# ScalarE fills a block's third PSUM bank before it copies the chain bank, two slopes move behind later additions, and one nested sum of w_in moves to the front

## The chip, the cores and the metric

The kernel runs on one core of a Trainium2 chip. A core has a matrix engine (TensorE, "PE" in the profile, with its weight loads shown apart as "PEld"), a vector engine (VectorE, "DVE"), a scalar engine (ScalarE, "ACT"), GpSimd ("POOL") and a queue engine (SyncE, "SP"). Each works through its own list of instructions in order; they wait for one another through semaphores. The metric is the time of one execution on the device in microseconds (us). Lower is better.

## The reference, cut to what matters

An attention whose mask comes from hash buckets makes `x`. A two-layer network with a leaky slope per hidden feature follows; that second part is what the change touches.

```python
# attn_out: softmax of q k^T / 8 where the 6-bit hash buckets of q and k agree, times v
x = attn_out.transpose(0, 2, 1, 3).reshape(3072, 512)
h = x @ w_in                                         # 512 -> 2048
g = np.maximum(h, 0.0) + alpha * np.minimum(h, 0.0)
return (g @ w_out).astype(np.float32)                # 2048 -> 512
```

`alpha` lies between 0 and 0.3, so `g` is the larger of `h` and `alpha * h`. In the kernel that is one VectorE instruction, called a slope below.

## The kernel before, in words

**Two parts.** The attention runs first, up to about 317 us into the profile. Then the two matrix products of the network run for four batches `b = 0..3` of 768 tokens. A hand-written loop over `blocks` (line 1598) takes, for each batch, eight blocks of kind "1" (the hidden layer, two feature tiles of 128 per block) and seven of kind "2" (the output layer). `do(...)` keeps instructions in the order in which the Python calls them, so the calls in this loop are the queues of the engines.

**Seven products in place of eight.** Each matrix product is cut 2 x 2 and computed with seven products of sums (a Strassen-like scheme). The class `Product` (line 906) holds one block. Its tiles are named by block and bank: `f_3a`, `f_3c` in the profile are PSUM banks "a" and "c" of hidden block 3, `f_3u` the SBUF copies of its chain, `z_7a` a bank of the output layer. Bank "a" is a chain: products are added on top of one another, and between two of them ScalarE copies the bank out (`keep`).

**Batches 1 to 3 nest the scheme.** There, three of the seven products of the hidden layer are computed for four blocks at once and once more by seven products. The class `Inner` (line 1105) does the first two (tiles `na` to `nf`, results `n`), the class `Third` (line 1172) the third (tiles `n_2a`, `n_2b`, `n_2c`; results straight into `g`). `unit(b, u, before)` (line 1248) runs both `Inner` products for blocks `4u..4u+3`. What is left of each block are four products, in the class `Rest` (line 1015). Its banks do not start at zero: ScalarE writes a first value into them, called a seed here.

**The steps of a `Rest` block**, each one call of `step`:

- step 1: ScalarE seeds bank "a" (one block ahead).
- step 6: PE adds a product to bank "a" (four matmuls, 384 wide); ScalarE copies it to tile `u1`.
- step 5: ScalarE seeds bank "c". PE does nothing.
- step 3: PE adds a product to bank "c", which needs the seed; VectorE adds "c" to `u1` in place (line 992) and takes the slope of the sum in place into `g` (line 996, reading `u1`), then one difference of `g` (line 977).
- step 7: PE adds to bank "a" (after the `u1` copy has been read out), ScalarE copies to `u2`, VectorE adds and takes a slope.
- step 4: PE adds the last product to "a"; ScalarE copies to `h`; VectorE takes the slope and one difference.

There is one buffer for bank "c" (its own PSUM pool) and one buffer for tile `u1`. So block n may seed "c" when VectorE's line 992 has read the "c" of block n-1, and may copy `u1` when VectorE's line 996 of block n-1 has read the old `u1`. At a block's change the loop calls

```python
                now = after
                now.step(6)
                third(b1, n1, "6")
                now.step(5)
                before.step(4)
```

which gives ScalarE the order: copy `u1`, copies of `Third`, seed "c", copy `h`. PE's order is step 6, `Third`, step 4 of the block before, then step 3.

**`Third`** is spread over the blocks by the table `THIRD` (line 1237). For blocks 4 to 7 its last step, 4, falls at the change to block 5; its VectorE work is one addition and `slopes(1)`, two slopes on `g` (line 1203).

**Sums of w_in.** The nested products need sums of quarters of `w_in` (`sum_inner`, line 1086: four additions, each followed by a store to DRAM on POOL's queue) and differences of quarters of `x` (`sum_inner_x`, line 1094: three). The sums of `w_in` are computed in batch 1 alone; later batches load them. In `unit` for `u = 0` VectorE's order is: three differences of `x`, then four sums of `w_in` (tiles `wp`), of which the second `Inner`'s step 5 (`nf<-xn,wp`) needs the first.

Of the kernel before, what the change touches and what calls it, by code (L numbers as in the profile page):

```python
# [407 lines left out]
def fast_path(  # L408
# [674 lines left out]
                do(nc.sync.dma_start(n_w[b, u, 2, 3 + m], w_n_s[u, 2, :, m]))  # L1083
            n_w[b, u, 2, 3 + m] = n_w[b, u, 2, 3 + m].rearrange("p (t f) -> p t f", t=2)

    def sum_inner(b, u, o):

        if b != 1:
            return
        for m, x, op, y in ((3, 21, ALU.add, 2), (4, 3, ALU.subtract, 0), (5, 0, ALU.subtract, 21), (6, 1, ALU.subtract, 4)):  # L1090
            do(DVE.tensor_tensor(n_w[b, u, o, m], n_w[b, u, o, x], n_w[b, u, o, y], op=op))
            nc.gpsimd.dma_start(w_n_s[u, o, :, m - 3].rearrange("p (t f) -> p t f", t=2), n_w[b, u, o, m])

    def sum_inner_x(b, o):

        x = x_m[b, (0, 3, 1)[o]]
        home = late[0] if o else mid
        t = home.tile([P, 4, HC], F32, name=f"xn{b}_{o}", tag=("x", "gs5", "m5")[o], bufs=1)
        left, right = (x[:, :, c * HC : (c + 1) * HC] for c in range(2))
        do(DVE.tensor_tensor(t[:, :2], right, x[:, 0].rearrange("p (c w) -> p c w", c=2), op=ALU.subtract))  # L1100
        do(DVE.tensor_tensor(t[:, 2], right[:, 1], t[:, 0], op=ALU.subtract))
        do(DVE.tensor_tensor(t[:, 3], left[:, 1], t[:, 2], op=ALU.subtract))
        n_x[b, o] = {0: left[:, 0], 1: left[:, 1], 2: right[:, 1], 3: t[:, 0], 4: t[:, 2], 5: t[:, 1], 6: t[:, 3]}
# [68 lines left out]
    class Third(Inner):  # L1172
# [30 lines left out]
                do(DVE.scalar_tensor_tensor(h, h, slope(i, False), h, op0=ALU.mult, op1=ALU.max))  # L1203

        def step(self, n):
            if n == 1:
                self.ps["a"] = two_banks(self.name + "a")[:, 0]
                self.ps["b"] = psum_bc[0].tile([P, 512], F32, name=self.name + "b", tag="b")
                self.times("a", 0, 0, True)
                do(ACT.copy(self.ps["b"][:, :CW], self.ps["a"][:, :CW]))  # L1210
            elif n == 2:
                self.times("b", 1, 1, False)
                self.add(0, 0, self.bank("b"))
            elif n == 6:
                self.times("a", 4, 4, False)
                self.keep("a", "u1")
                self.add(0, 1, self.sb["u1"])
            elif n == 5:
                self.ps["c"] = psum_bc[0].tile([P, 512], F32, name=self.name + "c", tag="b")
                self.times("c", 3, 3, True)  # L1220
                self.keep("c", "p5")
                self.add(1, 1, self.sb["p5"])
            elif n == 7:
                self.times("a", 5, 5, False)
                self.keep("a", "u2")
                self.add(1, 1, self.sb["u2"], self.to(1, 1))
            elif n == 3:
                self.times("c", 6, 2, False)
                self.add(0, 1, self.bank("c"), self.to(0, 1))
                self.slopes(0)  # L1230
            elif n == 4:
                self.times("a", 2, 6, False)
                self.add(1, 0, self.bank("a"))
                self.slopes(1)

    thirds = {}
    THIRD = (
# [4 lines left out]
    def third(b, i, place):  # L1242

        n = THIRD[i // 4].get((i % 4, place))
        if n:
            thirds[b, i // 4].step(n)

    def unit(b, u, before):

        def bank(name, tag=None):  # L1250
            name = f"n{name}{b}_{u}"
            return psum_bc[0].tile([P, 512], F32, name=name, tag=tag) if tag else two_banks(name)[:, 0]

        one = Inner(b, u, 0, bank("a"), bank("b", "b"), bank("c"))
        one.step(1)
        one.step(5)
        before.step(4)
        one.step(2)
        if not u:
            sum_inner_x(b, 1)  # L1260
        one.step(6)
        if not u:
            sum_inner(b, 0, 1)
            sum_x(b, 3, DVE)
        two = Inner(b, u, 1, bank("d"), bank("e", "b"), bank("f", "c"))
        two.step(1)
        one.step(3)
        two.step(5)
        one.step(7)
        if u:  # L1270
            sum_inner(b, 1, 2)
            sum_w2(b, 0, 3, 4)
        two.step(2)
        two.step(6)
        three = thirds[b, u] = Third(b, u)
        if u:
            three.step(1)
        one.step(4)
        two.step(3)
        if u:  # L1280
            three.step(2)
        now = ff1(b, 4 * u)
        now.step(1)
        two.step(7)
        now.step(6)
        now.step(5)
        two.step(4)
        three.step(6 if u else 1)
        if u:
            sum_w2(b, 0, 6, 5)  # L1290
        turn_out()
        if not u:
            sum_inner_x(b, 2)
            sum_inner(b, 0, 2)
        return now
# [302 lines left out]
    for j, (b, what, n) in enumerate(blocks):  # L1598
        n2 = n + 1 if what == "2" else 0 if n == NI - 1 else 7
        if n2 == 0:  # L1600
            sides_g(b, 0)
            if b == 0:
                sum_w2(b, 0, 3, 4)
        if not j:
            now.step(6)
        elif not (b and what == "1"):
            now.step(2)
        if j == 0:
            now.step(3)
            now.step(7)  # L1610
            now.step(2)
        if what == "2" and n == 6 and b + 1 < B:
            sum_inner(b + 1, 0, 0)
        now.step(22)
        if (b, what, n) == (1, "2", 1):
            largest()
        if what == "2" and b + 1 < B and 2 <= n < 6:
            if n == 3:
                sum_inner_x(b + 1, 0)
            else:  # L1620
                sum_x(b + 1, {2: 0, 4: 1, 5: 2}[n], DVE)
        if b and what == "1" and n == 1:
            load_inner(b, 1)
        if b and what == "1" and n == 2:
            load_third(b, 1)
        if b and what == "1" and n in (2, 3):
            sum_inner(b, 1, n - 2)
        if 0 < n2 < 7:
            sides_g(b, n2)
            sum_w2(b, n2, 3, 4)  # L1630
        if n2 < 7:
            sum_g2(b, n2, 3, 4)
        if j:
            if not (b and what == "1"):
                now.step(5)
                now.step(6)
            now.step(3)
            if b and what == "1":
                third(b, n, "3")
            if n2 or b == 0:  # L1640
                sum_w2(b, n2, 6)
            if b and what == "1" and (n + 1) % 4:
                after = ff1(b, n + 1)
                after.step(1)
            now.step(7)
            if b and what == "1":
                third(b, n, "7")
            if n2 or b == 0:
                sum_w2(b, n2, 5)
            sum_g2(b, n2, 5)  # L1650
        if (b, what, n) == (1, "2", 3):
            verdict()
        if what == "2" and n < 2:
            sum_g(1 + n)

        for n_out in [(), (0,), (1,), (2, 3), (4,), (5, 6), (7,)][j] if j < 7 else ():
            sum_out(n_out)
        for n_out in [(1,), (2, 3), (4,), (5, 6), (7,)][j] if j < 5 else ():
            load_out(n_out)
        if what == "1":  # L1660
            load_w(b * NI + n + 3)

            if b and n in (2, 5):
                load_w2(b, n // 4)
            if not b and n >= NI - 2:
                load_w2(b, n - NI + 2)
        else:
            load_w2(b, n + 2)
            if b + 1 < B:
                if n == 5:  # L1670
                    load_inner(b + 1, 0)
                    load_third(b + 1, 0)
                if n == 0:
                    load_x(b + 1)
        if j + 1 == len(blocks):
            turn_last(0)
        elif what == "1" or n < 6:
            turn_out()
        before = now
        if j + 1 < len(blocks):  # L1680
            b1, what1, n1 = blocks[j + 1]
            if b1 and what1 == "1" and n1 % 4 == 0:
                now = unit(b1, n1 // 4, before)
            elif b1 and what1 == "1":
                now = after
                now.step(6)
                third(b1, n1, "6")
                now.step(5)
                before.step(4)
                third(b1, n1, "4")  # L1690
            else:
                now = ff1(b1, n1) if what1 == "1" else ff2(b1, n1)
                now.step(1)
                before.step(4)
        else:
            before.step(4)
        if n2 < 7:
            sum_g2(b, n2, 6)
# [29 lines left out]
```

## Time and profile before

| what | value |
|---|---|
| median of 3 runs | 862.58 us (862.37 to 862.63) |
| the profiled execution | 862.93 us |
| its span in the trace | 861.1 us |
| granted PE clock | 0.998 of full speed |
| PE busy from 475 to 520 us (blocks 3 to 7 of batch 1) | 43.74 of 45.00 us |
| PE busy from 610 to 655 us (the same of batch 2) | 44.75 of 45.00 us |
| PE busy from 745 to 790 us (the same of batch 3) | 44.75 of 45.00 us |
| DVE busy in the same three stretches | 40.54, 37.91, 37.94 us |
| ACT busy in the same three stretches | 19.60, 20.51, 19.85 us |

The span runs from the first recorded instruction to the last; the execution takes 1.8 us more than it. The page gives no chain of waits for this kernel, so the argument has to come from the waits, the timeline and the starts of matmuls. Busy times of PE are modelled from starts and shapes; starts are recorded.

### The profile page before, as it was taken

What the parts mean: (1) busy time and instruction counts of PE and PEld (TensorE: products, weight loads), DVE (VectorE), ACT (ScalarE), POOL (GpSimd) and SP (SyncE); (2) the same over time, 40 slices, a digit from 0 to 9 for tenths busy, and PEclk for the clock granted to TensorE, in tenths of its full rate; (3) what the DMA queues carried; (4) which work ended last, traced back from release to release, by engine and by line L of the source; (5) the groups of instructions that cost most, each with busy time, mean ns of one, the idle gap of its engine ahead of it and who ended that gap; (6) DMA issues with size and microseconds to landing.
All of it is one profiled execution on the core that took longest, in us unless ns stands there. A gap on an engine that the chain in (4) does not pass through costs nothing.

```text
span 861.1 us, 15383 instructions
## 1 busy us (share of the span) xinstructions
PE 848.1 (98%) x5674; PEld 598.6 (70%) x5674; DVE 770.9 (90%) x1251; ACT 407.7 (47%) x754; POOL 154.5 (18%) x321
## 2 busy tenths in 40 slices
PE   8999999999999999999999999999999999999996
PEld 4444444444444445569997769999777999687996
DVE  6999999999999987899997989997879998879986
ACT  7777888877778833331124442114442114352111
POOL 1322433324334310210016200002100000300001
PEclk9999999999999999999999999999999999999999
DMA  8965779879597437774444744335833335830252
GB/s 197 180 149 132 187 177 251 170 197 256 131 241 194 154 117 258 250 260 176 148 151 122 271 135 136 110 118 177 290 125 113 144 117 171 264 115 20 99 166 60
DMA packets 181765, 144.85 MB, mean 168 GB/s; under 512 B 121536, under 2 KB 161648, under 8 KB 178096
## 3 DMA queue, kind: packets, MB, share of 16 engines
q1 hardware_dynamic: 166496, 113.15, 46.3%
q0 software_dynamic: 12176, 29.29, 11.2%
q10 hardware_dynamic: 3008, 1.33, 0.6%
q8 instruction: 47, 0.77, 0.4%
q14 instruction: 38, 0.31, 0.1%
HBM read 111.16 MB, written 31.46 MB: 166 GB/s over the span
## 4 chain that ended last, share of the span: by engine, by line


## 5 line engine op out<-in xcount | busy, mean ns | idle before, releaser
L790 ACT ACTIVATE pt<-sc 128x768 f32<-128x768 f32 x192 | 153.9, 813 | 3.2 <-PE sc L787 3.0
L787 PE MATMUL sc<-qT,kT 64*128 64x384 f32 x768 | 155.0, 482 | 0.0
L820 PE MATMUL av<-pt,vn 128*32 128x385 f32 (+1 forms) x1536 | 127.0, 485 | 0.0
L820 PEld LDWEIGHTS av<-pt,vn 128*32 128x32 f32 x1536 | 50.3, 109 | 73.8 <-issue 68.8
L787 PEld LDWEIGHTS sc<-qT,kT 64*128 64x128 f32 x768 | 68.2, 187 | 37.8 <-issue 37.6
L1407 POOL DMA_DIRECT2D out_dram<-o x52 | 28.3, 552 | 339.7 <-DVE o L1400 338.2
L787 PE MATMUL sc<-qb,kb 64*128 64x384 bf16 x384 | 63.0, 324 | 0.7 <-DVE alpha L563 0.4
L977 DVE TENSOR_TENSOR g<-g,g 128x768 f32<-128x768 f32 (+1 forms) x80 | 62.7, 792 | 0.7
L1353 DVE TENSOR_TENSOR gs<-g,gs 128x768 f32<-128x768 f32 x56 | 53.2, 951 | 1.0
L1353 DVE TENSOR_TENSOR gs<-g 128x768 f32<-128x768 f32 x56 | 53.2, 950 | 0.0
L1345 DVE TENSOR_TENSOR ws<-wl 128x512 f32<-128x512 f32 x56 | 38.3, 684 | 6.7 <-DMA wl<-w_out_s 6.7
L787 PEld LDWEIGHTS <-kb 64*128 64x128 bf16 x384 | 19.4, 94 | 34.9 <-issue 11.9
L607 ACT ACTIVATE wr<-raw 128x512 int32<-128x512 uint32 x32 | 22.1, 690 | 30.6 <-DVE wso L651 15.3
L748 POOL DMA_DIRECT2D qb<-hr x60 | 30.0, 507 | 25.9 <-ACT hr L743 25.9
L798 DVE TENSOR_TENSOR accp<-pt,pt 128x1536 f32<-128x1536 f32 x16 | 28.1, 1756 | 7.2 <-ACT pt L790 7.2
L996 DVE SCALAR_TENSOR_TENSOR g<-h,alpha 128x384 f32<-128x384 f32 x39 | 23.9, 613 | 6.4 <-ACT h L989 6.4
L803 DVE TENSOR_TENSOR accd<-accd,pt 128x1536 f32<-128x1536 f32 x16 | 28.1, 1759 | 1.7
L809 DVE TENSOR_TENSOR accd<-accd,accp 128x1536 f32<-128x1536 f32 x16 | 28.1, 1758 | 0.6
L806 DVE TENSOR_TENSOR accp<-accp,pt 128x1536 f32<-128x1536 f32 x16 | 28.0, 1753 | 0.0
L802 DVE TENSOR_TENSOR accd<-pt,pt 128x1536 f32<-128x1536 f32 x16 | 28.0, 1751 | 0.0
L1557 ACT ACTIVATE qT<-qT 128x768 f32<-128x768 f32 x15 | 12.7, 844 | 25.3 <-DMA kb<-hr 20.8
L1365 DVE TENSOR_TENSOR m<-m,m 128x768 f32<-128x768 f32 x24 | 22.7, 945 | 0.3
(494 smaller groups left out, 1903.9 us busy)
## 6 DMA issues: line engine op xcount, KB each, us to landing
wi<-w_in_s SPq DMA_DIRECT2D x32, 512.0 KB
wl<-w_out_s SPq DMA_DIRECT2D x16, 1024.0 KB
wl<-w_out_r SPq DMA_DIRECT2D x12, 1024.0 KB
raw<-in_moe_w_in_dram POOLq DMA_DIRECT2D x15, 512.0 KB, 5.1
raw<-in_moe_w_out_dram POOLq DMA_DIRECT2D x14, 512.0 KB, 4.8
w_in_s<-wsi SPq DMA_DIRECT2D x16, 448.0 KB
qn<-in_q_dram SPq DMA_DIRECT2D x64, 96.0 KB
vn<-in_v_dram SPq DMA_DIRECT2D x16, 384.0 KB
```

The source lines that it names most:

```text
L748: queue.dma_start(bits[name, pi][D * s : D * s + 2 * NB, half * CW : (half + 1) * CW], raw[c : c + 2 * NB],)
L787: do(PE.matmul(sc[:, s, :CW], what["k", pi][r, ks], what["q", pi][r, qs], start=first, stop=not first,))
L790: do(ACT.activation(pts[kc][:, g, :, :CW], sc[:, :, :CW], AF.Exp, scale=SCALE / DOWN))
L798: do(DVE.tensor_tensor(accp[pi], p(0), p(1), op=ALU.add))
L802: do(DVE.tensor_tensor(accd[pi], p(3), p(4), op=ALU.add))
L803: do(DVE.tensor_tensor(accd[pi], accd[pi], p(5), op=ALU.add))
L809: do(DVE.tensor_tensor(accd[pi], accd[pi], accp[pi], op=ALU.add))
L820: do(PE.matmul(av[pi][D * s + t : D * s + t + 32, g, :w], nat["v", pi][:, s, kc * D + t : kc * D + t + 32], pts[kc][:, g, s, :w], start=(k ...
L977: do(DVE.tensor_tensor(new_g(b, to)[:, at], g_m[b, x][:, at], g_m[b, y][:, at], op=ALU.subtract))
L1345: do(DVE.tensor_tensor(t, w2[b, n, x], w2[b, n, y], op=op))
L1353: do(DVE.tensor_tensor(t, g2[b, n, x], g2[b, n, y], op=ALU.subtract))
L1407: pinned(b + 1 < B and queue is nc.sync, queue.dma_start(out_v[b, ch * CH + c].rearrange("(w r) d -> r w d", r=32)[:, :, cols], src[32 * a ...
```

## The change

The function `sum_inner` takes a choice of sums, and `sum_inner_x` takes something to do after its first difference. In `unit` for `u = 0` the order on VectorE becomes: first difference of `x`, first sum of `w_in` (and its store on POOL's queue), the other two differences, the other three sums.

In `Third.step(4)` the two slopes are called for blocks 0 to 3 alone. For blocks 4 to 7 the loop calls them after step 7 of block 5, that is behind block 5's two additions (line 992), their slopes and one difference.

Steps 5 and 6 are exchanged at the change of every block but the first of four, and in `unit` for the first: ScalarE seeds "c" and then copies `u1`. PE's order stays.

```diff
-    def sum_inner(b, u, o):
+    def sum_inner(b, u, o, *ms):
...
         for m, x, op, y in ((3, 21, ALU.add, 2), (4, 3, ALU.subtract, 0), (5, 0, ALU.subtract, 21), (6, 1, ALU.subtract, 4)):
+            if ms and m not in ms:
+                continue
             do(DVE.tensor_tensor(n_w[b, u, o, m], n_w[b, u, o, x], n_w[b, u, o, y], op=op))
...
-    def sum_inner_x(b, o):
+    def sum_inner_x(b, o, between=lambda: None):
...
         do(DVE.tensor_tensor(t[:, :2], right, x[:, 0].rearrange("p (c w) -> p c w", c=2), op=ALU.subtract))
+        between()
         do(DVE.tensor_tensor(t[:, 2], right[:, 1], t[:, 0], op=ALU.subtract))
...
             elif n == 4:
                 self.times("a", 2, 6, False)
                 self.add(1, 0, self.bank("a"))
-                self.slopes(1)
+                if not u:
+                    self.slopes(1)
...
         if not u:
-            sum_inner_x(b, 1)
+            sum_inner_x(b, 1, lambda: sum_inner(b, 0, 1, 3))
         one.step(6)
         if not u:
-            sum_inner(b, 0, 1)
+            sum_inner(b, 0, 1, 4, 5, 6)
...
         two.step(7)
+        now.step(5)
         now.step(6)
-        now.step(5)
         two.step(4)
...
                 third(b, n, "7")
+                if n == 5:
+                    thirds[b, 1].slopes(1)
...
                 now = after
+                now.step(5)
                 now.step(6)
                 third(b1, n1, "6")
-                now.step(5)
                 before.step(4)
```

More of the change, by code (lines that the diff above doesn't have):

```diff
@@ L1205, in step @@
         def step(self, n):
+            b, u, o = self.key
             if n == 1:
```

## The prediction

> **What bounds the kernel now.** I read the page's busy times first, then PE's waits, then the timeline around each wait. The page:
>
> ```profile
> PE 848.1 (98%) x5674; PEld 598.6 (70%) x5674; DVE 770.9 (90%) x1251; ACT 407.7 (47%) x754; POOL 154.5 (18%) x321
> ```
>
> PE is busy nearly throughout, so what can be won without removing a product is only where PE stands still. PE's waits from 420 us on, in full:
>
> ```profile
> PE f_3c L928 <- ACT f_3c L1020: 1.0, 1, 1.0
> PE f_6c L928 <- ACT f_6c L1020: 0.8, 3, 0.3
> PE z_7a L928 <- DMA wl<-w_out_s: 0.4, 1, 0.4
> PE nf L1122 <- DVE wp L1091: 0.4, 1, 0.4
> PE z_4c L928 <- DVE m L1374: 0.2, 1, 0.2
> ```
>
> Columns: total, times, longest. Three of the five are what the change is about: seed "c" of block 3 (in batch 1 only), seed "c" of block 6 (once in each of batches 1 to 3), and the sum `wp` (batch 1). The times are too small, since PE's busy ends are modelled past the next start. The starts in the timeline give the loss. Block 3 of batch 1:
>
> ```profile
> 479.02 1.55 DVE L1091 TENSOR_TENSOR wn<-wn 128x256 f32<-128x256 f32 x4
> 480.23 1.45 PE L928 MATMUL f_2a<-x,wi 128*128 128x384 f32 x4
> 480.49 0.55 DVE L992 TENSOR_TENSOR f_2u<-f_2u,f_2c 128x384 f32<-128x384 f32 x1
> 481.07 0.62 DVE L996 SCALAR_TENSOR_TENSOR g<-f_2u,alpha 128x384 f32<-128x384 f32 x1
> 481.77 0.48 ACT L935 COPY f_3u<-f_3a 128x384 f32<-128x384 f32 x1 [2.10 <-PE f_2a L928]
> 482.15 0.49 ACT L1020 COPY f_3c<-n 128x384 f32<-128x384 f32 x1
> 482.69 1.56 PE L928 MATMUL f_3c<-x,wi 128*128 128x384 f32 x4 [1.01 <-ACT f_3c L1020]
> ```
>
> and block 6 of batch 1:
>
> ```profile
> 509.07 1.15 DVE L1203 SCALAR_TENSOR_TENSOR g<-g,alpha 128x384 f32<-128x384 f32 x2
> 510.14 0.55 DVE L992 TENSOR_TENSOR f_5u<-f_5u,f_5c 128x384 f32<-128x384 f32 x1
> 510.63 1.45 PE L928 MATMUL f_5a<-x,wi 128*128 128x384 f32 x4
> 510.72 0.62 DVE L996 SCALAR_TENSOR_TENSOR g<-f_5u,alpha 128x384 f32<-128x384 f32 x1
> 511.43 0.48 ACT L935 COPY f_6u<-f_6a 128x384 f32<-128x384 f32 x1 [1.40 <-DVE g L996]
> 511.80 0.49 ACT L1020 COPY f_6c<-n 128x384 f32<-128x384 f32 x1
> 512.35 1.56 PE L928 MATMUL f_6c<-x,wi 128*128 128x384 f32 x4 [0.26 <-ACT f_6c L1020]
> ```
>
> In both the reader is to see one chain: DVE's slope (L996) frees tile `u1`; only then ACT copies `u1`; only then ACT seeds "c"; only then PE starts. The seed itself needs only L992, which ended 0.6 us earlier. (For `f_3u` the view names PE as releaser, but that product was long done; the copy starts 0.08 us after L996 ends at 481.69.)
>
> Undisturbed, a chain of four 384-wide matmuls starts 1.29 us after the one before (the timeline has 477.65, 478.94, 480.23). So `f_3c` was due at 481.52 and started 1.17 us late; the chain behind it starts 1.39 instead of 1.29 us later (484.08), so 0.10 us more goes with the restart: **1.27 us**. `f_6c` was due at 511.92: 0.43 + 0.10 = **0.53 us**, and as much in batches 2 (646.42) and 3 (779.22): 3 x 0.53 = **1.58 us**. The sum:
>
> ```profile
> 453.17 0.55 DVE L1100 TENSOR_TENSOR xn<-x 128x384 f32<-128x384 f32 x1
> 454.42 0.42 DVE L1091 TENSOR_TENSOR wp<-wq 128x256 f32<-128x256 f32 x1
> 454.90 0.92 PE L1122 MATMUL nf<-xn,wp 128*128 128x192 f32 x4 [0.36 <-DVE wp L1091]
> ```
>
> Four 192-wide matmuls take 0.65 us from start to start; the chain before `nf` starts at 453.72, so `nf` was due at 454.37: 0.53 + 0.10 = **0.63 us**. The three together: 3.48 us, all that the change can address.
>
> **What the Trainium skill says.** "Perfetto Trace Analysis", section Identifying the Most-Contended Engine and the one after it on strategy: matmul busy time flatters PE because matmuls are pipelined, and one should look for gaps on the contended engine and for what releases them. The trace agrees: 0.26 us shown as idle is 0.53 us by the starts. "TensorE: Matmul & The Clock Gate", Part 3, The mechanism: matmuls start and end strictly in program order. So a chain that waits for a seed holds up all behind it; here the delay of `f_3c` reappears whole in `f_3a` (484.08). "ScalarE: Activation LUTs", Step-by-step, says that ScalarE writes faster to PSUM than to SBUF. This trace doesn't show it for these forms (seed into PSUM 489 ns, copy out to SBUF 479 ns), so I use 489 and 479.
>
> **Part 1, the nested sum first (batch 1 only).** Nothing is added; seven DVE instructions and the POOL stores behind the sums change places. The first difference ends at 453.72 and `wp` (0.42 us, independent of it) follows at about 453.7, so it ends near 454.1. `nf`'s weights would have been loaded from 454.21 on. The wait goes whole: gain 0.63. What is late next: the other sums keep their place or nearly so, and the next product with a sum, `nd` (456.95, due at 456.32 then), needs the second sum, which ends near 455.1. Its cover is 1.2 us. The POOL store is issued about 0.8 us earlier; what it feeds is read only in batch 2.
>
> **Part 2, seed before the copy.** No instruction is added; ACT, 47% busy, exchanges two of about 0.48 us in each of 24 blocks. At block 3 of batch 1, times of the old frame: L992 ends at 481.04, the seed starts at about 481.07 and ends at 481.56, the weight load begins 0.05 us later as now (482.64 to 482.69), at 481.61. A stalled first matmul takes 590 ns instead of 486, so the chain starts in effect at 481.61 + 0.10 = 481.71, and 0.2 us are lost in place of 1.27: gain 1.07. Bounds: 0.9 (DVE's queue reaches L992 0.15 us later) to 1.27 (the load hides in the chain before, as for `f_7c`, whose load comes 0.28 us late at no cost to PE). This needs DVE to follow PE's 0.63 us from part 1: DVE waited 0.73 us for ACT's copy of `f_1u` before 473.19, so it was tied to PE there and moves along.
>
> The exchange has a cost side: what stands behind the seed on ACT is the `u1` copy, a copy of `Third`, and `h`. The `u1` copy starts no earlier than before anyway, since L996 comes after L992; it is read by PE's step 7 only 1.29 us after the seeded chain has begun, and by DVE's L992 after that chain. In `unit`, the seed of `f_4c` needs L1163 (ends 496.40) and now stands behind `n_1u` (ends 497.10), 0.8 us ahead of the `f_4u` copy (497.90). I price it at nothing; without that cover each blocked copy would cost what DVE is late.
>
> **Part 3, the slopes later.** Two instructions, 1.15 us together, leave the place before L992 of block 5 and go behind its second slope. L992 then starts near 509.0 and ends near 509.55. With part 2 the seed of `f_6c` starts once the ACT copy of `f_5u` is out (510.03) and ends near 510.5; due is 511.92. Cover 1.4 us. Parts 2 and 3 each would do here alone: with part 2 alone the seed ends at 511.2; with part 3 alone L996 ends at 510.2, the copy follows PE's `f_6a` (510.8) and the seed ends near 511.75. Gain 3 x 0.53 = 1.58. DVE's sum of work before L992 of block 6 (514.65) stays, so the seed of `f_7c` can be out by 515.7 against a need of about 517.1 then. The features 6 and 7 of `g` that the slopes finish are first read in the output layer (`z_1b`, 522.78).
>
> **Sum.** 0.63 + 1.07 + 1.58 = 3.28 us. Whether it reaches the end: in the output layer of batch 1 DVE is never idle from 536.93 to beyond 580, and PE waits for it at `z_4c` (0.50 us by the starts). But DVE itself waited 0.69 us at 536.93 for a load of `w_out`, issued at 532.07, when PE's chain freed the buffer (chain start 530.6 plus 1.3). So that stretch hangs on PE and moves with it; likewise `z_7a`'s wait for a load. Batches 2 and 3 show DVE gaps of 0.5 to 2 us in every unit, and the last loads of batch 3 (DVE gap 2.58 before 832.34) are issued behind stores that DVE's transposes start. I take no loss here; bounds: a loss of up to batch 1's whole 2.2 us, or a gain of 0.5 if `z_4c`'s wait shrinks. Profiled execution: 862.93 - 3.28 = 859.65 (span 857.8); against the median 862.58, which lies 0.35 lower: 859.3.
>
> **The rivals.**
>
> - *Block 3 stays late (gain about 2.2, 860.4).* If DVE doesn't move with PE between 473 and 480, part 1's 0.63 comes back as wait at `f_3c`, or the seed finds L992 late by some 0.5 us more. For: DVE has no gap from 473.19 to 491.5. Against: the 0.73 us gap just before.
> - *Batch 1's gain is absorbed (gain about 1.05, 861.5).* DVE's unbroken stretch to 580, with the `z_4c` wait at its end, may give back all 2.2 us if the `w_out` loads don't come earlier; only the `f_6c` of batches 2 and 3 then count, 2 x 0.53. For: PE does wait for DVE and DMA there. Against: the loads are issued as PE frees their buffers.
> - *Slower: ACT's head is blocked.* Place: the seed in front of the `u1` copy in all 24 blocks. If a seed waits for DVE beyond the time at which PE needs the copy behind it, PE's next chain in "a" stands. It begins to cost once DVE's L992 is later than about 1.3 us after the `u1` product; at 0.2 us in each of 24 blocks it costs 4.8, net +1.5: 864.1. For: ACT is strictly in order, DVE is 84 to 90% busy there. Against: the seed's chain is due before that copy's reader in every block.
>
> **How the numbers follow.** Forecast (all three parts, 858.7 to 860.0) 0.62; block 3 late 0.15; absorbed 0.14; slower 0.09. What this measurement can tell from no change is about 0.2%, 1.7 us; so faster is the first two, 0.77, within is the third, 0.14, slower 0.09. The range goes from 858.6 (forecast with a shorter `z_4c` wait) to 861.2, which takes in block 3 late and part of the absorbed case: about 0.8.
>
> **What would show it.** In the changed profile PE's waits have no `f_6c` and no `nf`; `f_3c` has at most 0.1 us. ACT's order at a block's change is seed, then `u1`. L1203 stands after L996 of block 5. `z_7a` and `z_4c` wait as before. The prediction is wrong if `z_4c` or `z_7a` grow by what was won, or if waits of "a" chains for ACT copies appear.

## The result, and the profile after

The changed kernel takes 859.48 us (median of 6 runs, 858.73 to 860.18) against 862.61 us for the kernel before, measured beside it (862.29 to 863.93). The ratio is 0.9961, 95% interval 0.9948 to 0.9974: 0.4% faster. Predicted was 859.3 us. The profiled execution took 859.58 us, its span is 857.8 us (before: 861.1).

The page of the changed kernel, busy times (engine, us, share of the span, instructions):

```profile
span 857.8 us, 15369 instructions
PE 848.8 (99%) x5674; PEld 599.4 (70%) x5674; DVE 770.6 (90%) x1251; ACT 408.3 (48%) x754; POOL 154.2 (18%) x321
```

PE does the same 5674 matmuls. Their busy time, which is modelled, is 0.7 us more, and the span is 3.3 us shorter. PE's waits of the changed kernel from 420 us on, in full:

```profile
PE z_4c L928 <- DVE m L1379: 0.3, 1, 0.3
```

`f_3c`, `f_6c` and `nf` have left the list. The changed kernel is a few lines longer: its L1093, L1102, L1125 and L1206 are L1091, L1100, L1122 and L1203 of the kernel before. Block 3 of batch 1 in the timeline of the changed kernel:

```profile
478.98 1.55 DVE L1093 TENSOR_TENSOR wn<-wn 128x256 f32<-128x256 f32 x4
480.19 1.45 PE L928 MATMUL f_2a<-x,wi 128*128 128x384 f32 x4
480.44 0.55 DVE L992 TENSOR_TENSOR f_2u<-f_2u,f_2c 128x384 f32<-128x384 f32 x1
481.02 0.48 ACT L1020 COPY f_3c<-n 128x384 f32<-128x384 f32 x1 [1.39 <-DVE f_2u L992]
481.03 0.62 DVE L996 SCALAR_TENSOR_TENSOR g<-f_2u,alpha 128x384 f32<-128x384 f32 x1
481.56 0.94 PEld L928 LDWEIGHTS f_3c<-x,wi 128*128 128x128 f32 x4 [0.53 <-ACT f_3c L1020]
481.56 1.56 PE L928 MATMUL f_3c<-x,wi 128*128 128x384 f32 x4
481.73 0.48 ACT L935 COPY f_3u<-f_3a 128x384 f32<-128x384 f32 x1 [0.23 <-PE f_2a L928]
```

The seed now starts 0.03 us after L992 has ended (480.99), no longer behind the `u1` copy. The weight load is still late by a little: the chain was due at 480.19 + 1.29 = 481.48, began at 481.56, and its second matmul again follows 0.10 us later than usual. 0.18 us remain of 1.27. The list of waits doesn't show them at all, since the loss falls below what the modelled ends can tell.

Block 6 of batch 1, the same view:

```profile
507.36 0.55 DVE L1200 TENSOR_TENSOR g<-n_2a,n 128x384 f32<-128x384 f32 x1
507.83 0.55 DVE L992 TENSOR_TENSOR f_5u<-f_5u,f_5c 128x384 f32<-128x384 f32 x1
508.79 0.49 ACT L1020 COPY f_6c<-n 128x384 f32<-128x384 f32 x1
509.51 1.45 PE L928 MATMUL f_5a<-x,wi 128*128 128x384 f32 x4
509.71 0.48 ACT L935 COPY f_6u<-f_6a 128x384 f32<-128x384 f32 x1 [0.43 <-PE f_6a L928]
510.80 1.45 PE L928 MATMUL f_6c<-x,wi 128*128 128x384 f32 x4
510.94 1.14 DVE L1206 SCALAR_TENSOR_TENSOR g<-g,alpha 128x384 f32<-128x384 f32 x2
```

The seed ends at 509.28 for a chain that starts at 510.80, 1.29 us after the one before: nothing is lost, and the seed is 1.5 us ahead. And the nested product with its sum:

```profile
453.88 0.55 DVE L1102 TENSOR_TENSOR xn<-x 128x384 f32<-128x384 f32 x1
454.31 0.81 PE L1125 MATMUL nc<-x,wn 128*128 128x192 f32 x4
454.35 0.42 DVE L1093 TENSOR_TENSOR wp<-wq 128x256 f32<-128x256 f32 x1
454.96 0.81 PE L1125 MATMUL nf<-xn,wp 128*128 128x192 f32 x4
```

`wp` follows the first difference at once and ends at 454.77; `nf` starts 0.65 us after `nc`, as it should.

To add up, I take every start of a matmul in the two matrix products and count what exceeds the undisturbed distance (322 ns behind a 384-wide matmul, 163 ns behind a 192-wide one). Two places with the same loss in both kernels are left out: 0.28 us at 320 us and 0.08 us near 850 us. In us, each figure rounded by itself:

| PE's loss at | before | after |
|---|---|---|
| `nf`, batch 1 | 0.63 | 0 |
| `f_3c`, batch 1 | 1.28 | 0.18 |
| `f_6c`, batches 1 to 3 | 1.57 | 0 |
| `z_7a`, `z_7c`, `z_4c`, batch 1 | 1.16 | 1.01 |
| `z_4a` before batch 1; `nc`, `nd` of its first unit | 0 | 0.44 |
| sum | 4.63 | 1.63 |

The first three rows fall by 3.28 us. The 0.44 us in the fifth row are no part of the change: they stand ahead of its first effect, and they are absent in a second profile of the same kernel (below).

That the span, too, is 3.3 us shorter is in part luck. From the first matmul of batch 1's nested products to the start of PE's last matmul the time falls from 404.40 to 401.25 us, by 3.15: that is the table without `z_4a`. The stretch ahead of it is 0.3 us longer, and the stretch behind it 0.43 us shorter (7.49 and 7.06 us). Over the twelve profiles of this case these two vary from 448.5 to 449.5 and from 7.0 to 7.7 us.

### The profile page after: what moved, and what is told of

Its sections match the earlier page's. It is cut to its first block, busy times and chain, and to the rows that moved or that the text cites. A ratio compares the mean times of both kernels' runs of the same rounds, so it can differ in the third digit from the quotient of the medians.

```text
span 857.8 us, 15369 instructions
## 1 busy us (share of the span) xinstructions
PE 848.8 (99%) x5674; PEld 599.4 (70%) x5674; DVE 770.6 (90%) x1251; ACT 408.3 (48%) x754; POOL 154.2 (18%) x321
## 4 chain that ended last, share of the span: by engine, by line
## 5 line engine op out<-in xcount | busy, mean ns | idle before, releaser
L996 DVE SCALAR_TENSOR_TENSOR g<-h,alpha 128x384 f32<-128x384 f32 x39 | 23.9, 614 | 5.2 <-ACT h L989 4.9
```

## The experiments

Two theories were set against each other. The first: each wait of PE costs what its starts say, DVE follows PE between two waits, and so the parts add. The rival: DVE is a bound of its own in batch 1, and what one wait gives back comes up at the next. The times are medians, each with the ratio and its 95% interval; the ratio is to the kernel before on the same chip. "Loss" is the count by starts described above.

**Part 1 alone** (`sum_first_only`): the kernel before with

```diff
-            sum_inner_x(b, 1)
+            sum_inner_x(b, 1, lambda: sum_inner(b, 0, 1, 3))
...
-            sum_inner(b, 0, 1)
+            sum_inner(b, 0, 1, 4, 5, 6)
```

> The kernel before with part 1 alone (first sum of w_in after the first difference of x). Theory (each of PE's waits costs what its matmul starts say, and DVE moves along with PE between two waits): PE's wait at nf goes, 0.63 us; f_3c stays 1.27 us late and the three f_6c 0.53 us each; 862.6 - 0.6 = 862.0 us. Rival (DVE is a bound of its own in batch 1, what is won comes back at the next wait): nf goes, but f_3c grows to 1.9 us; 862.6 us, no change. In the profile: loss at f_3c by matmul starts 1.3 or 1.9 us.

Measured: 862.1 us, ratio 0.9992 (0.9985 to 0.9999). PE's waits:

```profile
PE f_3c L928 <- ACT f_3c L1020: 1.0, 1, 1.0
PE f_6c L928 <- ACT f_6c L1020: 0.8, 3, 0.3
PE z_4c L928 <- DVE m L1377: 0.3, 1, 0.3
PE z_7c L928 <- DVE m L1377: 0.2, 1, 0.2
```

`nf` is gone and `f_3c` loses 1.27 us, not 1.9: DVE came forward with PE in the 27 us between the two. The rival falls here.

**Part 2 alone** (`seed_first_only`): the kernel before with

```diff
                 now = after
+                now.step(5)
                 now.step(6)
                 third(b1, n1, "6")
-                now.step(5)
```

and the same exchange in `unit`.

> The kernel before with part 2 alone (ScalarE seeds bank c and then copies u1). Theory: f_3c falls from 1.27 to about 0.2 us, the three f_6c from 0.53 to 0, nf keeps its 0.63; gain 1.07 + 1.58 = 2.65, 860.0 us. Rival that the later slopes are what frees f_6c: the f_6c keep about 0.5 us each, gain 1.1, 861.5 us. Rival that DVE's backlog takes it back in the output layer of batch 1: z_4c and z_7a lose 1.6 us more, gain 1.05, 861.5 us.

Measured: 859.54 us, ratio 0.9963 (0.9950 to 0.9977). Loss: `nf` 0.63, `f_3c` 0.18, no `f_6c`; the three waits in the output layer 1.37 together. At block 6 of batch 1, with the two slopes still in their old place:

```profile
508.62 0.55 DVE L992 TENSOR_TENSOR f_5u<-f_5u,f_5c 128x384 f32<-128x384 f32 x1
509.20 0.48 ACT L1020 COPY f_6c<-n 128x384 f32<-128x384 f32 x1 [0.69 <-DVE f_5u L992]
510.41 1.45 PE L928 MATMUL f_6c<-x,wi 128*128 128x384 f32 x4
```

The seed ends 0.7 us ahead of its chain. So part 2 by itself removes the stalls at both seeds. The time was lower than expected and equal to that of the whole change, although `nf` still costs; that was taken up again below.

**Part 3 alone** (`slopes_later_only`): the kernel before with

```diff
-                self.slopes(1)
+                if not u:
+                    self.slopes(1)
...
                 third(b, n, "7")
+                if n == 5:
+                    thirds[b, 1].slopes(1)
```

> The kernel before with part 3 alone (two slopes behind step 7 of block 5). Theory: L996 of block 5 ends 1.15 us earlier, the u1 copy then follows PE's f_6a, the seed is out about 0.15 us before its chain is due: the three f_6c lose at most 0.1 us each; f_3c keeps 1.27, nf 0.63; gain 1.3 to 1.6, 861.1 us. Rival (only the seed's place in ACT's queue counts): the f_6c keep 0.5 us each, 862.6 us.

Measured: 860.88 us, ratio 0.9979 (0.9970 to 0.9987). Loss: `f_3c` 1.27, `nf` 0.62, no `f_6c`. Block 6 of batch 1 in its timeline:

```profile
510.62 1.45 PE L928 MATMUL f_5a<-x,wi 128*128 128x384 f32 x4
510.82 0.48 ACT L935 COPY f_6u<-f_6a 128x384 f32<-128x384 f32 x1 [0.81 <-PE f_6a L928]
511.19 0.49 ACT L1020 COPY f_6c<-n 128x384 f32<-128x384 f32 x1
511.73 1.01 PEld L928 LDWEIGHTS f_6c<-x,wi 128*128 128x128 f32 x4 [0.28 <-ACT f_6c L1020]
511.91 1.45 PE L928 MATMUL f_6c<-x,wi 128*128 128x384 f32 x4
```

The copy is still ahead of the seed, but it now waits for PE and not for DVE. The weights are loaded 0.28 us late, 0.18 us before the matmul is due, and the chain starts on time (510.62 + 1.29 = 511.91).

**The change without part 2** (`copy_first_again`): the changed kernel with

```diff
-                now.step(5)
                 now.step(6)
                 third(b1, n1, "6")
+                now.step(5)
```

and the same in `unit`.

> The changed kernel with part 2 undone (ScalarE copies u1 and then seeds c); parts 1 and 3 stay. Theory: f_3c is late by 1.27 us again, nf and f_6c stay at 0 to 0.1; 859.5 + 1.1 = 860.6 us. Rival that part 2 carries all of it: f_6c 0.5 us each again, 862.2 us. Rival that part 2 has no share of its own: 859.5 us.

Measured: 860.25 us, ratio 0.9969 (0.9958 to 0.9980). Loss: `f_3c` 1.27, no `nf`, no `f_6c`; the output layer of batch 1 loses 1.27, of which 1.05 at `z_7a`. Block 3 belongs to part 2 alone; block 6 is freed by part 2 or by part 3, whichever is there.

**The seed still earlier** (`seed_a_block_early`): the changed kernel with

```diff
                 after = ff1(b, n + 1)
                 after.step(1)
+                after.step(5)
...
                 now = after
-                now.step(5)
                 now.step(6)
```

> The changed kernel with the seed of bank c moved still further ahead, behind the seed of bank a of the next block (that is in front of the u2 copy of the block that runs). It tests what the slower rival said: a seed that waits for DVE's L992 holds up what stands behind it on ACT. Theory (it costs where DVE is behind, and only there): the u2 copy comes late and with it PE's step 4 of the same block: about 1.9 us at block 2 of batch 1, 0.5 at block 2 of batches 2 and 3, 0.4 at block 6 of all three, nothing at the other blocks, f_3c's 0.2 goes; 859.5 + 3.8 = 863.3 us. Rival (ACT at 48% busy has room, the order within it costs nothing as long as the seed is early): 859.3 us.

Measured: 862.9 us, ratio 1.0003 (0.9994 to 1.0011): the whole gain is given back. Block 2 of batch 1 in its timeline:

```profile
478.10 1.45 PE L928 MATMUL f_3a<-x,wi 128*128 128x384 f32 x4
479.64 0.55 DVE L992 TENSOR_TENSOR f_2u<-f_2u,f_2c 128x384 f32<-128x384 f32 x1
480.23 0.48 ACT L1020 COPY f_3c<-n 128x384 f32<-128x384 f32 x1 [3.64 <-DVE f_2u L992]
480.64 0.47 ACT L935 COPY f_2u<-f_2a 128x384 f32<-128x384 f32 x1
481.17 1.56 PE L928 MATMUL f_2a<-x,wi 128*128 128x384 f32 x4 [1.62 <-ACT f_2u L935]
```

ACT stands 3.64 us at the head of its queue for a seed that DVE hasn't freed. Behind it waits the `u2` copy, whose bank PE had filled 2.4 us before, and PE waits for that. Loss: 1.88 at block 2 of batch 1, 0.42 in each of batches 2 and 3, 0.35 at block 6 of all three, nothing at the other blocks, and `f_3c`'s 0.18 is gone; expected were 1.9, 0.5 and 0.4. So the slower rival's mechanism is real, with a price; the change escapes it because the copy that it moves the seed past, `u1`, could not run before L996 anyway.

**The small DVE work out of batch 1's output layer** (`verdict_in_batch3`): the changed kernel with

```diff
-        if (b, what, n) == (1, "2", 1):
+        if (b, what, n) == (3, "2", 1):
             largest()
...
-        if (b, what, n) == (1, "2", 3):
+        if (b, what, n) == (3, "2", 3):
             verdict()
```

> The changed kernel with the thirteen small VectorE instructions of largest and verdict (2.0 us together in batch 1's output layer) and their one transpose moved to the same place of batch 3. Theory (PE's waits z_7a, z_7c and z_4c of batch 1, 1.0 us by the starts, come from DVE's unbroken stretch there; batch 3 has DVE gaps up to 2.5 us): they fall to 0.2 us or less together and nothing new comes in batch 3; 859.5 - 0.8 = 858.7 us. Rival (the loads of w_out set these waits): z_7a and z_4c stay, 859.5 us. Rival (batch 3 has no room): the same wait appears there, 859.5 us or more.

Measured: 858.37 us, ratio 0.9955 (0.9942 to 0.9969). Loss in the output layer of batch 1: `z_7a` 0.07, `z_4c` 0.23, no `z_7c`, 0.30 together in place of 1.01, and none in batch 3. That is more than the 0.2 us expected; what sets the rest stays open. So most of the wait there is DVE's backlog, and batch 3 has the room.

**And the sums `wn` later** (`verdict_and_wn_later`): in addition

```diff
-        if b and what == "1" and n in (2, 3):
-            sum_inner(b, 1, n - 2)
+        if b and what == "1" and n == 3:
+            sum_inner(b, 1, 1)
...
                 third(b, n, "3")
+                if n == 2:
+                    sum_inner(b, 1, 0)
```

> The same as the kernel with the verdict in batch 3, and in batch 1 the four sums wn of block 2 go behind block 2's step 3 (its addition L992, slope and difference), so that L992 comes 1.5 us earlier. Theory: the seed of f_3c is out in time, its remaining 0.18 us goes, the sums are still ahead of nc<-xn,wn; 858.7 - 0.2 = 858.5 us. Rival (the sums come too late for the nested product): PE waits at nc for DVE's sum, 0.5 us or more, 859 us or more.

Measured: 858.53 us, ratio 0.9955 (0.9941 to 0.9969). `f_3c` loses nothing and no wait appears at `nc`:

```profile
477.76 0.55 DVE L992 TENSOR_TENSOR f_2u<-f_2u,f_2c 128x384 f32<-128x384 f32 x1
478.35 0.48 ACT L1020 COPY f_3c<-n 128x384 f32<-128x384 f32 x1
479.75 1.55 DVE L1093 TENSOR_TENSOR wn<-wn 128x256 f32<-128x256 f32 x4
480.26 1.45 PE L928 MATMUL f_3c<-x,wi 128*128 128x384 f32 x4
```

The four sums in front of L992 were what was left there. The output layer of batch 1 loses 0.39 in place of 0.30, so by the starts 0.10 of the 0.18 us stay. That can't be told in the time, which is that of the kernel above within its spread. The medians of both lie below the changed kernel's, with overlapping intervals.

**Does part 1 last?** Three kernels side by side.

> The changed kernel unaltered, on the same chip as the next two, because the time of part 2 alone (859.54 us) stood no higher than that of the whole change (859.48) in separate measurements, while the starts of matmuls say that 0.63 us at nf separate them. Theory: 859.3 us, and by the starts neither nf nor f_6c lose anything; the 0.16, 0.15 and 0.14 us lost at z_4a, nc and nd in its first profile do not come back.

> Part 2 alone once more. Theory: 0.63 us at nf remain, so 0.5 to 0.7 us above the whole change on the same chip, 859.9 us. Rival (part 1 earns nothing that lasts): the same time as the whole change.

> The kernel before with parts 1 and 2, without the later slopes. Theory: with the seed in front of the copy the slopes' place is worth nothing, so no f_6c loses anything and the time is that of the whole change within 0.2 us, 859.3 us. Rival (part 3 has a share of its own): up to 0.5 us above it.

Measured, in this order: 859.04 us (0.9957, 0.9944 to 0.9971), 859.6 us (0.9964, 0.9951 to 0.9978), 859.77 us (0.9961, 0.9947 to 0.9974). The whole change stands 0.56 us ahead of part 2 alone, but the intervals overlap, and parts 1 and 2 together are no faster than part 2 alone by their medians. The traces say why. The next table cuts each span in three: up to the first matmul of batch 1's nested products, from there to the start of PE's last matmul, and the rest.

| profile, us | ahead | between | behind |
|---|---|---|---|
| the kernel before | 449.17 | 404.40 | 7.49 |
| the change, in the result | 449.48 | 401.25 | 7.06 |
| the change, again | 448.86 | 400.98 | 7.34 |
| part 2 alone, again | 448.91 | 401.72 | 7.41 |
| parts 1 and 2 | 449.41 | 401.34 | 7.27 |

"Parts 1 and 2" starts half a microsecond late, before any part of the change acts. In the stretch between, part 1 is worth 0.38 us on top of part 2 (401.72 to 401.34) and 0.76 by itself (404.40 to 403.64 in its own profile). `nf`'s 0.62 to 0.63 us are in both, and the rest is the output layer of batch 1, which loses 1.14 and 1.38 in the first pair, 1.16 and 1.02 in the second. So part 1 earns its 0.63 us by the starts, and the output layer adds or takes up to 0.24. The times of whole executions are almost too coarse for it: of part 1 alone the interval ends just below 1, at 0.9999.

Parts 1 and 2 lack 0.36 us to the whole (401.34 against 400.98), and all of it is that output layer: 1.38 against 1.03. Whether the later slopes cause it stays open: in two profiles of part 2 alone the same sum was 1.37 and 1.14. The 0.44 us at `z_4a`, `nc` and `nd` did not come back.

## Why the prediction was right

- *What bounds the kernel.* PE, from batch 1 to its last matmul: that stretch is shorter by 3.15 us in the first profile and by 3.42 in the second, against 3.28 us for the three waits. The difference is `nc` and `nd` in the first and the output layer in both; no other gap opened.
- *Part 1*, predicted 0.63 us: `nf`'s loss went from 0.63 to 0. That it isn't lost at the next wait is shown by part 1 alone, where `f_3c` kept its 1.27.
- *Part 2 at block 3*, predicted 1.07 with 0.2 left: 1.09, with 0.18 left, and 0.18 to 0.19 in all six kernels with that order in which the sums `wn` stand in front of L992. The step from L992 over the seed to the weight load is as worked out. That the remainder is the four sums `wn` in front of L992 is shown by moving them.
- *Block 6*, predicted 1.58: 1.57. That parts 2 and 3 each suffice is shown by each alone. The seed is out 1.5 us ahead of its chain where both are there, 0.7 with part 2 alone and 0.2 with part 3 alone. For `f_6c` the later slopes are thus a second remedy for a cured wait.
- *No loss in the output layer.* "`z_7a` and `z_4c` wait as before" held for the sum and not for the places: 1.16 us before, 1.01 after, and between 1.02 and 1.38 in the other kernels with the verdict in batch 1. It shifts between `z_7a`, `z_7c` and `z_4c`. The absorbing rival had named the right place, a DVE without a gap, but that stretch hangs on PE at its beginning, so an earlier PE pulls it along: the load of `w_out` issued at 532.07 left at 530.42 in the changed kernel, and the DVE instruction that waits for it came forward from 536.93 to 535.12.
- *The slower rival* needed DVE to be later than the copy behind the seed can bear. It is, once the seed stands one copy further forward in the queue: 3.4 us, the whole gain.
- The time, 859.3 against 859.48 measured and 859.04 in the second measurement, is nearer than the method can promise: two profiles of the changed kernel differ by 0.6 us before batch 1 begins and by 0.3 us behind PE's last matmul. That much of the match is luck.

## What to carry to other kernels

In an in-order queue, an instruction that fills a buffer for the busiest engine belongs ahead of one whose release comes later, even if the two are independent: what is lost is the difference of the two releases and the time of the instruction in front. At block 3 that was 0.70 us from where the seed could have started (481.07, 0.03 us behind L992) to the start of the copy (481.77), and 0.38 us from there to the start of the seed. Find both releases in the timeline, and what stands behind the instruction that is moved: moved one copy further, the same seeds cost as much as the whole change had earned. Price a stall from the starts of matmuls (late start plus slower restart), and compare kernels between two common events, one just ahead of the change and one at the end of the busiest engine's work, since what lies outside scatters by as much as such a gain.

## What the runs showed of the hardware

- A chain of matmuls whose weight load came late pays a second time. Behind its first matmul the second starts 0.43 us later in place of 0.32 (384 wide), or 0.27 in place of 0.16 (192 wide). The extra 0.10 to 0.11 us don't depend on how late the chain was: `f_3c` paid them at 0.08 us (the change) and at 1.17 us (before), and `z_7c` at 0.01 us (part 2 alone, again).
- They go with how far the weight load starts ahead of its matmul. With both at the same time (within 2 ns) the extra was 0.10 to 0.11 us; with the load 0.03 us ahead 0.08 (`z_4a` at the end of batch 3, in all twelve profiles); 0.04 us ahead 0.07 (`z_7a` with the verdict in batch 3); 0.18 us ahead nothing (`f_6c` with part 3 alone, after a wait of 0.28 us for the seed). So a wait of the weight load alone is a warning and not yet a loss.
- ScalarE's copies of 128x384 values take 463 ns from PSUM to PSUM (`ne<-nd`), 479 from PSUM to SBUF (`f_3u<-f_3a`) and 489 from SBUF to PSUM (the seeds) in the profile before. The prediction set 489 against 479 and saw no advantage of PSUM as a destination. With the source the same, 463 against 479, there is one of 16 ns; the seeds are slower because of their source or of something that goes with it.
